# w3 times w_out summed row by row in all eight PSUM banks, and the first unit's gates put ahead of the rounding

## The chip, the cores and the metric

The kernel runs on one core of a Trainium2 chip. The metric is the device time of one execution in microseconds (us). The core has five engines with a queue each: TensorE (PE; its weight loads are shown apart as PEld), VectorE (DVE), ScalarE (ACT), GpSimd (POOL) and SyncE (SP), which here issues all the DMAs. Within one queue, instructions run in the order in which they were built.

## The reference

A gated linear recurrence over the sequence is followed by a feed-forward block without a nonlinearity.

```python
# q, k, v, a_re, a_im: (B=4, H=8, S=768, D=48); S_re, S_im: states of D x D for each head
mag = np.sqrt(a_re * a_re + a_im * a_im)
scale = np.minimum(mag, 0.999) / (mag + 1e-06)
a_re_n, a_im_n = (a_re * scale, a_im * scale)
for t in range(S):
    new_re = ar * S_re - ai * S_im
    new_im = ar * S_im + ai * S_re
    kv = np.einsum('bhd,bhe->bhde', k[:, :, t], v[:, :, t])
    S_re, S_im = (new_re + kv, new_im)
    y[:, :, t] = np.einsum('bhd,bhde->bhe', q[:, :, t], S_re)
# x: y with the heads beside each other, (3072, 384)
a = x @ w1              # (384, 1024)
b = x @ w2              # (384, 1024)
h = a * b @ w3          # (1024, 1024)
return (h @ w_out)      # (1024, 384)
```

The four weights come as 64-bit floats, everything else as 32-bit floats.

## The kernel before

**Units.** The sequences are cut into eight units of work, two halves of 384 steps (TT) for each of the four batches; a unit has three chunks of 128 steps. Each unit has two sides. Its gates (`gates`, L529 on) are elementwise: ACT and DVE turn re and im into running products of magnitudes and running sums of angles, and multiply them into q and k. The results are moved (L630) into the tiles KL and QL, which have heads in another place; twelve DMAs a unit. Then PE does the attention of the unit: transposes of the keys (`turn`, L650, copied out by ACT in L652), scores of a chunk (`scores`, L662, masked by DVE in L664), outputs (`outputs`, L689, copied by ACT to xT in L691) and states (`state`, L700, added up by DVE in L707). Two of the tiles, re and im, exist once, so that the next unit's loads wait for the last reader.

**The feed-forward block.** `ffn_ab` (L720) multiplies x by a block of w1 and one of w2, ACT copies the first (L725) and DVE multiplies (L726). Since nothing stands between w3 and w_out, the kernel multiplies those two once, into w3o (1024 by 384), and `ffn_out` (L736) multiplies by that. While PE does the attention of one unit, it does the feed-forward work of the unit before.

**Rounding.** 64-bit weights are loaded as pairs of 32-bit words into raw tiles of 8 KB a partition (three of them) and rounded to 32-bit floats by `convert`. For w3: two passes on ACT (L762, L764) and two on DVE (L766, L773). For the others: one on ACT (L768) and three on DVE (L769, L771, L773). ACT's result goes to the tile low, of which there is one.

**The start.** PE's order is written out by hand at the end of the function (a manual schedule); for the other engines the order comes from a scheduler that goes by the order of the program and by priority. The program loads the first column block of w3 in two halves, then the gates' inputs of unit 0, then w_out in four blocks of two rows, and then seven more column blocks of w3, each with 1 KB pieces. `fuse(j)` multiplies column block j by w_out in eight matmuls into one PSUM bank, in two parts of four, and ACT copies the bank to w3o (L847). Each of these matmuls is two in the trace. A column block needs all of w_out, so the first matmul of a block runs as soon as the rows it needs are rounded. Steps of the gates of unit 0 are put between the blocks. Blocks 0 to 5 go first on PE; blocks 6 and 7 are put as fill between the pieces of unit 0's attention.

**PSUM.** Eight banks are given out by name: two for scores (ps_s, tag sc), two for transposes, outputs and states (ps_v, tag v), four for the feed-forward block and for fuse (ps_m, tag mm).

**SP.** All loads and moves stand in one queue. A load of a raw tile waits until the rounding three loads before has read its tile.

Of the kernel before, what the change touches and what calls it, by code (L numbers as in the profile page):

```python
# [10 lines left out]
FP = mybir.dt.float32  # L11
# [4 lines left out]
AF = mybir.ActivationFunctionType  # L16
# [358 lines left out]
def kernel(  # L375
# [36 lines left out]
    nc = tc.nc  # L412
    B, H, D, S = qt.shape
    P = 128
    C = 128
    NC = S // C
    DM = H * D
    FF = w1.shape[1]
    KD = DM // P
    DG = P // H  # L420
    KF = FF // P
    WB = 2 * P
    HEAD = 6
    SPLIT1 = False
    TT = S // 2
    UC = TT // C
    NU = 2 * B
# [9 lines left out]
    w3o = weights_pool.tile([P, KF, DM], FP, name="w3o")  # L437
# [6 lines left out]
    one = fast.enter_context(tc.tile_pool(name="one", bufs=1))  # L444
    two = fast.enter_context(tc.tile_pool(name="two", bufs=2))
    ps_s = fast.enter_context(tc.tile_pool(name="ps_s", bufs=2, space=PSUM))
    ps_v = fast.enter_context(tc.tile_pool(name="ps_v", bufs=2, space=PSUM))
    ps_m = fast.enter_context(tc.tile_pool(name="ps_m", bufs=4, space=PSUM))
# [31 lines left out]
    def load_rows(dst, src, u, which=range(KD), queue=nc.sync):  # L480
        b, h = divmod(u, 2)
        for i, f in enumerate(which):
            queue.dma_start(out=dst[:, i, 0:TT], in_=src[b, :, DG * f:DG * (f + 1), h * TT:(h + 1) * TT].rearrange(
                "h d s -> d h s"))

    def load_gates(u):
        g = g_t.setdefault(u, {})
        for n, src in (("re", art), ("im", ait)):
            g[n] = one.tile([P, KD, TT], FP, tag=n, name=n)
            load_rows(g[n], src, u)  # L490

    def take_qk(u):
        g = g_t.setdefault(u, {})
        g["q"] = gate_pool[u % 2].tile([P, KD, TT], FP, tag="q", name="q")
        g["k"] = gate_pool[u % 2].tile([P, KD, TT + 1], FP, tag="k", name="k")

    def load_qkv(u):
        b, h = divmod(u, 2)
        if "q" not in g_t.get(u, {}):
            take_qk(u)  # L500
        g = g_t[u]
        load_rows(g["k"], kt, u)
        load_rows(g["q"], qt, u)


        vr = one.tile([P, UC, DM], FP, tag="vr", name="vr")
        nc.sync.dma_start(out=vr, in_=v[b, h * TT:(h + 1) * TT].rearrange("(c p) e -> p c e", p=C))
        g["vr"] = vr
# [20 lines left out]
    def gates(u, split):  # L529
# [6 lines left out]
        re, im, q = g["re"], g["im"], g["q"]  # L536
        K2 = g["k"]
        k, r = K2[:, :, 0:TT], R[:, :, 0:TT]
        parts = [slice(0, KD)]

        def act(**kw):
            chain(nc.scalar.activation(**kw))  # L542
# [55 lines left out]
        for s in parts:  # L598
            for f in range(s.start, s.stop):
                nc.vector.tensor_tensor_scan(  # L600
                    out=Z[:, f], data0=im[:, f], data1=im[:, f],
# [3 lines left out]
        for s in parts:  # L605
            n = re[:, s].bitcast(I32)
# [146 lines left out]
    def convert(dst, src, halves):  # L753
        r, m = dst.shape[1:]
        raw = cv["raw"].tile([P, r, m, 2], I32, tag="raw", name="raw")
        nc.sync.dma_start(out=raw.rearrange("p r m w -> p r (m w)"), in_=src)
        lo, hi = raw[:, :, :, 0], raw[:, :, :, 1]
        low = cv["low"].tile([P, r, m], I32, tag="low", name="low")
        b = dst.bitcast(I32)
        if halves:  # L760
            ends = low.rearrange("p r m -> p (r m)")
            nc.scalar.activation(out=ends.bitcast(U16)[:, 0::2].rearrange("p (r m) -> p r m", r=r), in_=lo.bitcast(U32),  # L762
                                 func=AF.Copy, scale=2.0 ** -29)
            nc.scalar.activation(out=ends.bitcast(BF)[:, 1::2].rearrange("p (r m) -> p r m", r=r), in_=hi.bitcast(FP),  # L764
                                 func=AF.Sign)
            nc.vector.tensor_scalar(out=b, in0=hi, scalar1=3, scalar2=None, op0=OP.logical_shift_left)  # L766
        else:
            nc.scalar.activation(out=low, in_=lo.bitcast(U32), func=AF.Copy, scale=2.0 ** -29)  # L768
            nc.vector.tensor_scalar(out=b, in0=hi, scalar1=3, scalar2=0x3FFFFFFF, op0=OP.logical_shift_left,  # L769
                                    op1=OP.bitwise_and)  # L770
            nc.vector.scalar_tensor_tensor(out=b, in0=hi, scalar=-0x40000000, in1=b, op0=OP.bitwise_and,  # L771
                                           op1=OP.bitwise_or)
        nc.vector.tensor_tensor(out=b, in0=b, in1=low, op=OP.add)  # L773

    def load_weight(dst, src, halves=False):
        if src.dtype == FP:
            nc.sync.dma_start(out=dst, in_=src)
        else:
            convert(dst, src, halves)

    def words(src):
        return (src if src.dtype == FP else src.bitcast(I32)).rearrange("(i p) m -> p i m", p=P)
# [27 lines left out]
    w3_t = {}  # L810

    def rounding():

        stack = ExitStack()
        for n, k in (("raw", 3), ("low", 1)):
            cv[n] = stack.enter_context(tc.tile_pool(name=n, bufs=k))
        return stack

    def columns(src, j0, j1):
        n = 1 if src.dtype == FP else 2  # L820
        return words(src)[:, :, n * j0:n * j1]
# [2 lines left out]
        return [lambda d=d, w=w, n=n: load_weight(d[:, n], columns(w, n * WB, (n + 1) * WB))  # L824
                for n in range(FF // WB) for d, w in ((w1s, w1), (w2s, w2))]

    def wo_work():
        w3_t["wo"] = one.tile([P, KF, DM], FP, tag="ab", name="wo_s")
        return [lambda i=i: load_weight(w3_t["wo"][:, i:i + 2], words(wo)[:, i:i + 2]) for i in range(0, KF, 2)]

    def w3_work(j, step=KF):
        w3_t[j] = two.tile([P, KF, P], FP, tag="xT", name="w3s")
        for f in range(0, KF, step):
            load_weight(w3_t[j][:, f:f + step], columns(w3t, j * P, (j + 1) * P)[:, f:f + step], True)

    def fuse(j):

        got = {}

        def part(f0):  # L840
            if f0 == 0:
                got["m"] = ps_m.tile([P, DM], FP, tag="mm", name="f")
            m = got["m"]
            for f in range(f0, f0 + KF // 2):
                nc.tensor.matmul(out=m, lhsT=w3_t[j][:, f], rhs=w3_t["wo"][:, f], start=(f == 0), stop=(f == KF - 1))  # L845
            if f0:
                nc.scalar.activation(out=w3o[:, j], in_=m, func=AF.Copy, scale=1.0 if w3t.dtype == FP else 2.0)  # L847
        return [lambda: part(0), lambda: part(KF // 2)]

    def judge():  # L850

# [50 lines left out]
    with tc.manual_schedule(engines={mybir.EngineType.PE}):  # L902

        phase = rounding()
        w3_work(0, KF // 2)
        load_gates(0)
        take_qk(0)
        steps = gates(0, True)
        for i, f in enumerate(wo_work()):
            f()  # L910
            if i >= 1:
                next(steps)
        w3_work(1)
        fill = fuse(0)
        for j in range(2, KF):
            if j == KF - 1:
                for _ in range(2):
                    next(steps, None)
            w3_work(j)
            if j == 2:  # L920
                load_qkv(0)
            for f in fill:
                f()
            fill = fuse(j - 1)
            next(steps, None)
            next(steps, None)
        work = w12_work()
        for f in work[:2]:
            f()
        for _ in steps:  # L930
            pass
        fill += fuse(KF - 1)
        load_gates(1)
        steps = gates(1, False)
        take_qk(1)
        rest = ffn(0, 2)
        work = work[2:]
        for i, p in enumerate(pieces(0)):
            for f in p:
                f()  # L940
            if i in (0, 1, 3, 5):
                fill.pop(0)()
            if i == 0:
                for f in work[:2]:
                    f()
                load_qkv(1)
            if i >= 2:
                next(steps)
            if i in (5, 7):
                work[2 + (i == 7)]()  # L950
        for i, f in enumerate(rest[:HEAD]):
            f()
            if i < 2:
                work[4 + i]()
            if i == 2:
                phase.close()
            next(steps)
        head_pool[1] = fast.enter_context(tc.tile_pool(name="late_heads", bufs=1))
        for _ in steps:
            pass  # L960
        load_gates(2)
        late = fast.enter_context(tc.tile_pool(name="late", bufs=2))
        look = check_weights(late)
        for u in range(1, NU):
            steps = gates(u + 1, False) if u + 1 < NU else iter(())
            unit(u, steps, rest[HEAD:] if u == 1 else ffn(u - 1), look if u > 1 else iter(()))
            for _ in steps:
                pass
            if u + 2 < NU:
                load_gates(u + 2)  # L970
        for _ in look:
            pass
        judge()
        for f in ffn(NU - 1):
            f()
# [41 lines left out]
```

## Time and profile before

| | us |
|---|---|
| median of 3 runs | 602.62 |
| lowest, highest | 602.47, 604.31 |
| the profiled execution | 604.26 |
| its span, from the first to the last instruction | 602.5 |
| PE busy | 554.6 (92%) |
| ACT busy | 345.4 (57%) |
| DVE busy | 300.0 (50%) |
| matmuls of w3 and w_out (L845), 128 of them | 46.7 |
| first of these matmuls starts | 17.16 |
| moves of unit 0 issued | 51.56 to 63.1 |
| first scores of unit 0 | 67.81 |
| first matmul with w1 | 95.44 |
| first scores of unit 1 | 136.03 |

The busy time of an engine is an average over stages with different limits, so a table by stage says more. In such a table a window of the span has one row, with the busy time of each engine. A view of waits says which instruction an engine stood waiting for. The chain of waits is followed back from the last instruction: at each step to what released it, or to the instruction before it on its engine. Matmuls are pipelined, and a matmul's duration is longer than the spacing from one to the next.

### The profile page before, as it was taken

What the parts mean: (1) busy time and instruction counts of PE and PEld (TensorE: products, weight loads), DVE (VectorE), ACT (ScalarE), POOL (GpSimd) and SP (SyncE); (2) the same over time, 40 slices, a digit from 0 to 9 for tenths busy, and PEclk for the clock granted to TensorE, in tenths of its full rate; (3) what the DMA queues carried; (4) which work ended last, traced back from release to release, by engine and by line L of the source; (5) the groups of instructions that cost most, each with busy time, mean ns of one, the idle gap of its engine ahead of it and who ended that gap; (6) DMA issues with size and microseconds to landing.
All of it is one profiled execution on the core that took longest, in us unless ns stands there. A gap on an engine that the chain in (4) does not pass through costs nothing.

```text
span 602.5 us, 8758 instructions
## 1 busy us (share of the span) xinstructions
PE 554.6 (92%) x3514; PEld 366.1 (61%) x3514; DVE 300.0 (50%) x388; ACT 345.4 (57%) x542; POOL 5.3 (1%) x11
## 2 busy tenths in 40 slices
PE   0599697959998999999999999999999999999996
PEld 0255584538755666667667766676567666766553
DVE  5988388744953664348324672477049602210110
ACT  5789476437484965588658986998375312101100
POOL 3000000000000000000000000000000000000000
PEclk9989898998999999999999999999999999999999
DMA  9996996373067268545744459735700430000001
GB/s 296 289 308 193 281 272 216 104 176 101 27 150 204 62 184 208 184 154 173 194 145 146 142 172 253 226 119 159 182 15 1 111 73 14 1 14 28 0 1 44
DMA packets 53025, 84.70 MB, mean 141 GB/s; under 512 B 4592, under 2 KB 44272, under 8 KB 52976
## 3 DMA queue, kind: packets, MB, share of 16 engines
q1 hardware_dynamic: 52976, 84.06, 49.1%
q8 instruction: 29, 0.48, 0.4%
q14 instruction: 20, 0.16, 0.1%
HBM read 60.42 MB, written 4.72 MB: 108 GB/s over the span
## 4 chain that ended last, share of the span: by engine, by line
PE 74%; DVE 9%; ACT 7%; DMA 5%; issue 2%; SPq 2%; ACTq 0%; DVEq 0%
PE m L720 36%; PE o L736 19%; PE sc L662 6%; PE y L689 5%; PE kv L700 4%; PE f L845 3%; DMA raw<-in_w_dram 2%; PE tp L650 2%; DMA QL<-q 2%; ACT re L542 1%; ACT gZ L542 1%; SPq L630 1%; ACT gR L542 1%; DVE w3s L773 1%; DMA look<-in_a_re_dram 1%
## 5 line engine op out<-in xcount | busy, mean ns | idle before, releaser
L720 PE MATMUL m<-xT,w1s 128*128 128x384 f32 x384 | 137.5, 495 | 5.3 <-ACT xT L691 5.3
L720 PE MATMUL m<-xT,w2s 128*128 128x384 f32 x384 | 134.3, 486 | 0.0
L736 PE MATMUL o<-w3o,ab 128*128 128x384 f32 x384 | 128.3, 489 | 0.0
L726 DVE TENSOR_TENSOR ab<-m,a 128x384 f32<-128x384 f32 x64 | 35.4, 554 | 150.5 <-PE m L720 141.0
L720 PEld LDWEIGHTS m<-xT,w2s 128*128 128x128 f32 x384 | 73.0, 190 | 51.0 <-issue 0.3
L736 PEld LDWEIGHTS o<-w3o,ab 128*128 128x128 f32 x384 | 71.4, 190 | 47.2 <-issue 1.4
L720 PEld LDWEIGHTS m<-xT,w1s 128*128 128x128 f32 x384 | 70.0, 192 | 46.6 <-ACT xT L691 6.5
L725 ACT COPY a<-m 128x384 f32<-128x384 f32 x64 | 30.4, 476 | 88.3 <-PE m L720 88.2
L845 PE MATMUL f<-wo_s,w3s 128*128 128x384 f32 x128 | 46.7, 518 | 21.7 <-DVE wo_s L773 19.3
L662 PE MATMUL sc<-QL,KL 96*128 96x128 f32 x384 | 51.2, 290 | 13.0 <-DMA QL<-q 10.0
L662 PEld LDWEIGHTS sc<-QL,KL 96*128 96x128 f32 x384 | 48.7, 202 | 19.7 <-issue 16.5
L845 PEld LDWEIGHTS f<-wo_s,w3s 128*128 128x128 f32 x128 | 24.8, 200 | 40.9 <-DVE wo_s L773 21.6
L652 ACT COPY KT<-tp 128x384 f32<-128x384 f32 x40 | 33.9, 848 | 26.3 <-PE tp L650 26.2
L664 DVE COPY_PREDICATED A<-causal,sc 128x512 f32<-128x512 int32 x48 | 34.0, 733 | 25.2 <-PE sc L662 24.8
L689 PE MATMUL y<-A,V 128*32 128x128 f32 x768 | 39.2, 275 | 0.6 <-DVE T L707 0.6
L689 PEld LDWEIGHTS y<-A,V 128*32 128x32 f32 x768 | 32.7, 109 | 9.4 <-issue 7.2
L689 PE MATMUL y<-QL,T 96*32 96x128 f32 x640 | 34.5, 272 | 0.0
L740 ACT COPY ot<-o 128x384 f32<-128x384 f32 x24 | 11.4, 476 | 40.1 <-PE o L736 40.1
L700 PEld LDWEIGHTS kv<-V,KT 128*96 128x96 f32 x320 | 29.8, 165 | 3.2 <-issue 1.8
L689 PEld LDWEIGHTS y<-QL,T 96*32 96x32 f32 x640 | 31.2, 110 | 0.0
L700 PE MATMUL kv<-V,KT 128*96 128x64 f32 x320 | 29.9, 246 | 0.0
L803 ACT ACTIVATE look<-look 128x512 f32<-128x512 f32 (+1 forms) x36 | 23.3, 654 | 10.3 <-DMA look<-in_w_dram 9.7
(98 smaller groups left out, 572.9 us busy)
## 6 DMA issues: line engine op xcount, KB each, us to landing
look<-in_w_dram SPq DMA_DIRECT2D x28, 512.0 KB, 4.8
raw<-in_w_dram SPq DMA_DIRECT2D x7, 1024.0 KB, 6.6
raw<-in_w_dram SPq DMA_DIRECT2D x8, 768.0 KB, 7.8
KL<-gR SPq DMA_DIRECT2D x24, 192.5 KB, 3.1
KL<-k SPq DMA_DIRECT2D x24, 192.5 KB, 3.8
re<-in_a_re_dram SPq DMA_DIRECT2D x24, 192.0 KB, 4.6
im<-in_a_im_dram SPq DMA_DIRECT2D x24, 192.0 KB, 3.9
k<-in_k_dram SPq DMA_DIRECT2D x24, 192.0 KB, 4.6
```

The costliest lines, as they stand in the source:

```text
L542: chain(nc.scalar.activation(**kw))
L652: nc.scalar.copy(out=KT_t[u, c][:, :, :, x].rearrange("p h d f -> p f d h"), in_=tp.rearrange("p f (d h) -> p f d h", h=H))
L662: nc.tensor.matmul(out=sc[:, j], lhsT=KL[:, x * n + j, w], rhs=QL[:, x * n + j, w], start=True, stop=True)
L664: nc.vector.copy_predicated(out=A[:, x * n:(x + 1) * n], data=sc, mask=causal.rearrange("p (h t) -> p h t", h=1).to_broadcast([P, n, C]))
L689: nc.tensor.matmul(out=o, lhsT=a, rhs=b, start=s0, stop=s1)
L700: nc.tensor.matmul(out=kv[:, hd], lhsT=KT[:, hd].rearrange("p d x f -> p (d x f)"), rhs=V[:, hd], start=True, stop=True)
L720: nc.tensor.matmul(out=m, lhsT=w[:, j * P // WB, f, j * P % WB:j * P % WB + P], rhs=xT_t[u][:, f], start=(f == 0), stop=(f == KD - 1))
L725: nc.scalar.copy(out=a, in_=got[0])
L726: nc.vector.tensor_tensor(out=ab_t[u][:, j], in0=got[1], in1=a, op=OP.mult)
L736: nc.tensor.matmul(out=m, lhsT=ab_t[u][:, f, t * P:(t + 1) * P], rhs=w3o[:, f], start=(f == 0), stop=(f == KF - 1))
L803: nc.scalar.activation(out=hi, in_=hi, func=AF.Square, scale=2.0 ** 15)
L845: nc.tensor.matmul(out=m, lhsT=w3_t[j][:, f], rhs=w3_t["wo"][:, f], start=(f == 0), stop=(f == KF - 1))
```

## The change

The multiplication of w3 and w_out is summed over rows instead of column blocks. A row of w3 here is a block of 128 partitions with all 1024 columns, 8 KB in one piece for each partition. `row_work(f)` loads and rounds row f of w3 and row f of w_out (384 columns, so that w_out comes in eight loads instead of four). The first row of w3 comes in two halves with w_out's row between them. `fuse(f, j)` is now one product: it adds row f's part to sum j. Eight sums are open at the same time, in all eight banks: two of tag sc, two of tag v and four of tag mm. Only after row 7 are they copied to w3o.

On PE, rows 0 to 5 go first with all eight products, then rows 6 and 7 with the products of sums 0 to 3; the products of rows 6 and 7 for sums 4 to 7 are the fill between the pieces of unit 0's attention, two at a time, at the same four places as before. The steps of unit 0's gates are emitted with high priority, two after each row, and all that are left before the last products; the copies to w3o have high priority too. The tile low has two buffers. The name SPLIT1, which nothing read, is replaced by SPLIT, an empty tuple, with which `parts` stays one slice.

```diff
-    SPLIT1 = False
+    SPLIT = ()
...
-        for n, k in (("raw", 3), ("low", 1)):
+        for n, k in (("raw", 3), ("low", 2)):
...
+    def row_work(f, parts=1):
+
+        if f == 0:
+            w3_t["wo"] = one.tile([P, KF, DM], FP, tag="ab", name="wo_s")
+        w3_t[f] = two.tile([P, FF], FP, tag="xT", name="w3s")
+
+        def some(n):
+            step = FF // parts
+            load_weight(w3_t[f][:, n * step:(n + 1) * step].rearrange("p (i m) -> p i m", i=1),
+                        columns(w3t, n * step, (n + 1) * step)[:, f:f + 1], True)
+        some(0)
+        load_weight(w3_t["wo"][:, f:f + 1], words(wo)[:, f:f + 1])
+        for n in range(1, parts):
+            some(n)
...
+    def fuse(f, j):
+        if not sums:
+            sums.extend([ps_s.tile([P, DM], FP, tag="sc", name="f") for _ in range(2)] +
+                        [ps_v.tile([P, DM], FP, tag="v", name="f") for _ in range(2)] +
+                        [ps_m.tile([P, DM], FP, tag="mm", name="f") for _ in range(4)])
+        nc.tensor.matmul(out=sums[j], lhsT=w3_t[f][:, j * P:(j + 1) * P], rhs=w3_t["wo"][:, f], start=(f == 0),
+                         stop=(f == KF - 1))
+        if f == KF - 1:
+            with tc.high_priority():
+                nc.scalar.activation(out=w3o[:, j], in_=sums[j], func=AF.Copy, scale=1.0 if w3t.dtype == FP else 2.0)
...
-        w3_work(0, KF // 2)
+        row_work(0, 2)
         load_gates(0)
         take_qk(0)
         steps = gates(0, True)
-        for i, f in enumerate(wo_work()):
-            f()
-            if i >= 1:
-                next(steps)
-        w3_work(1)
-        fill = fuse(0)
-        for j in range(2, KF):
-            if j == KF - 1:
-                for _ in range(2):
+        for f in range(KF):
+            if f:
+                row_work(f)
+            if f == 2:
+                load_qkv(0)
+            if f >= KF - 2:
+                continue
+            for j in range(KF):
+                fuse(f, j)
+            for _ in range(2):
+                with tc.high_priority():
                     next(steps, None)
-            w3_work(j)
-            if j == 2:
-                load_qkv(0)
-            for f in fill:
-                f()
-            fill = fuse(j - 1)
-            next(steps, None)
-            next(steps, None)
         work = w12_work()
         for f in work[:2]:
             f()
-        for _ in steps:
-            pass
-        fill += fuse(KF - 1)
+        with tc.high_priority():
+            for _ in steps:
+                pass
+        for f in range(KF - 2, KF):
+            for j in range(KF // 2):
+                fuse(f, j)
+        fill = [lambda f=f, j=j: [fuse(f, j + x) for x in range(2)] for f in range(KF - 2, KF) for j in range(KF // 2, KF, 2)]
```

As built, SP's queue has the loads of rows 0 to 5 first, with unit 0's inputs between them and, after row 4, the loads of unit 1's im and k and a third of its q; then the twelve moves of unit 0; and only then the loads of rows 6 and 7 and of w1 and w2. Before, all of w3 and the first block of w1 stood ahead of the moves, and unit 1's inputs behind them. On ACT and DVE the two last gate stages of unit 0 stand ahead of the rounding of rows 5 to 7. From the moves of unit 1 on, the order of loads is the same as before.

More of the change, by code (lines that the diff above doesn't have):

```diff
@@ L538, in gates @@
         k, r = K2[:, :, 0:TT], R[:, :, 0:TT]
-        parts = [slice(0, KD)]
+        parts = [slice(f, f + 1) for f in range(KD)] if u in SPLIT else [slice(0, KD)]
         def act(**kw):
@@ L825, in w12_work @@
                 for n in range(FF // WB) for d, w in ((w1s, w1), (w2s, w2))]
[L827 to L848, printed above, removed]
+    def row_work(f, parts=1):
[10 more added lines that the diff above has]
+            some(n)
+    sums = []
+    def fuse(f, j):
[8 more added lines that the diff above has]
+                nc.scalar.activation(out=w3o[:, j], in_=sums[j], func=AF.Copy, scale=1.0 if w3t.dtype == FP else 2.0)
     def judge():
```

## The prediction

> **What bounds the kernel now.** I read the busy table first, then a table by stage, the waits of PE, and the chain of waits.
>
> ```profile
> 29.00:60.00 31.00, 30.65 (x91) 17.79 (x92) 25.75 (x35) 28.45 (x32) 0.00 (x0) 0.94 0.81 251
> 60.00:68.00 8.00, 3.39 (x14) 1.88 (x13) 2.52 (x3) 2.13 (x3) 0.00 (x0) 1.00 1.05 280
> 68.00:96.00 28.00, 23.39 (x285) 20.00 (x285) 20.34 (x27) 17.27 (x22) 0.00 (x0) 0.93 1.05 292
> ...
> 136.00:186.00 50.00, 45.78 (x375) 32.72 (x376) 28.84 (x32) 30.34 (x45) 0.00 (x0) 0.96 0.42 109
> 186.00:602.00 416.00, 410.62 (x2638) 271.62 (x2636) 173.48 (x224) 229.65 (x396) 0.00 (x0) 1.00 0.40 113
> ```
>
> Columns: window, length, busy PE, PEld, DVE, ACT, POOL, granted clock, DMA share, GB/s. From 186 us on PE is full, with work that the change leaves alone. A gain can only come from making that stage start earlier.
>
> ```profile
> PE f L845 <- DVE wo_s L773: 19.3, 4, 17.2
> PE sc L662 <- DMA QL<-q: 10.0, 2, 5.4
> PE m L720 <- ACT xT L691: 5.3, 2, 4.0
> PE sc L662 <- DMA out_dram<-ot: 3.0, 1, 3.0
> ```
>
> These are PE's waits (total, times, longest). Two are for QL: unit 0's scores at 67.81 and unit 1's at 136.03.
>
> ```profile
> 62.57 5.00 DMA QL<-q
> 67.81 3.53 PE sc L662 x16
> ...
> 86.25 7.77 DMA raw<-in_w_dram
> 94.11 0.91 ACT low L768
> 95.44 13.53 PE m L720 x36
> ...
> 116.66 1.37 DVE gZ L608
> ...
> 131.15 4.58 DMA QL<-q
> 136.03 3.75 PE sc L662 x16
> ```
>
> The chain passes through unit 0's moves, a w1 block, and then unit 1's gates. From 94 to 115.6 us DVE idles about 1 us in all, so those gates share a full DVE with the last four w1/w2 blocks. Everything after 136 us hangs on that QL: unit 2's re is loaded behind unit 1's moves and starts unit 2's gates, whose QL holds PE again at 185. So the end follows the instant at which unit 1's gates finish, not the instant at which unit 0's do.
>
> **What the Trainium skill says.** "DMA: Bandwidth & Descriptors", section "Anatomy of one DMA": semaphore waits are taken by the issuing sequencer, and DMA engines only consume their queues. The trace agrees: SP stood 10.8 us in five waits for L766, with everything behind it unissued. Same page, "Specifications": 512 B and more run at line rate, so 1 KB pieces should lose nothing against 8 KB. The trace differs a little: 1 KB pieces of w3 ran at 348 GB/s (34 to 40 us), 3 KB pieces of w_out at about 400 (11 to 14 us). "TensorE: Matmul & The Clock Gate", "HAM oscillation": idle gaps above some 3.4 us bring the slow clock back. It agrees: after 4.6 us idle the 16 score matmuls took 3.53 us, after 2.95 us idle 2.02. "PSUM — Partial Sum Buffer", "The four PSUM rules": an output fills at most one of eight banks; eight open sums leave none for a transpose. No trace here shows that yet.
>
> **The change, step by step.** I replay the changed kernel's built instruction order by hand, with the spacing of like instructions in this trace: L762 and L764 1.21 us each (a w3 row 2.42 on ACT), L766 0.6, L773 1.15; gate passes of 1152 elements 1.07 on ACT, 1.27 on DVE; a scan 0.93; KT copy 0.65; L768 0.82; a move's issue 0.62.
>
> Unknown first: a 384-element w_out rounding. On DVE it costs at least half of the 768 form (2.3/2 = 1.15 us) and at most all of it (2.3). I take 1.35, so eight rows cost 1.6 more than four pairs (0 to 9). The cover is the 8 us in which DVE waits for row 6, below; without it that 1.6 lands in the gates. The second low buffer lets ACT run a row ahead (three waits on L773, 3.3 us in all, in the view of raw); it is in the replay. SPLIT replaces an unused name: nothing.
>
> *Gates of unit 0.* ACT gets r0a, wo0, r0b, then re, which 0.39 MB of w_out has pushed from at most 8.35 to about 9.3. L762 of row 1 stands before the first gZ pass and waits for row 1 (about 14.0), so that pass goes from 13.54 to 15.2, and the Exp before the scans ends at 22.7 (20.44 before). From there the rounding steps aside: scans end 26.2 (27.6), Arctan starts 30.0 (36.7), L600 ends 35.2 (43.0), the last Sin ends 44.0 (54.4). The twelve moves are issued from 43.6 to 51.9 (51.56 to 63.1). Eleven us are won for unit 0.
>
> *And given back.* On SP the load of row 6 stands behind all twelve moves, although its raw slot is free near 42. Issued at 52.0 behind 2.4 MB of moves (250 GB/s, as at 62 to 66 us), it lands at 58.5. With three raw slots shared by rows of w3 and w_out, row 7 lands at 62.2 and the last w_out row at 64. ACT, idle from 49 to 58.5, ends row 7 at 64.9, DVE at 66.6. PE has rows 6 and 7 for four sums (8 x 0.65 = 5.2 us) ahead of its first transpose, and the transposes and scores need banks that only the w3o copies free: row 7's four matmuls end 69.2, the fourth copy 69.7. With 0.35 per transpose and 1.3 per pair of fills, scores start at 72.6 instead of 67.81, with 2.6 us of fills left instead of 5.2. PE is 2.2 us behind at this place. Behind the waiting transpose stand all of PE; behind the waiting w3o copies on ACT stand KT, low of w2 and unit 1's first Ln.
>
> *Unit 1.* Its im, k and a third of q were loaded early (1.4 MB), but rows 6 and 7 (2.9 MB) now fall into the busy stretch. From the moves' end to the last needed w1 block 11.7 MB have to land: 2.9 MB of rows at 400 GB/s (done at 63.2, bound by their issues), 8.85 MB at the 290 of 68 to 96 us: 30.5 us, plus 1.5 to land: 95 (94.05 for an earlier block before). ACT runs from 69.7 nearly without a gap: 22 operations, about 18 us, plus some 3.5 of waits for w1/w2 blocks, vr and L567. Unit 1's Exp before the scans ends 91.2 (87.6), L574 stands behind unit 0's third A and T on DVE and ends 93.8. The third xT comes at 96.2 behind that block, PE m at 96.3 (95.44).
>
> But of the four late w1/w2 blocks two were rounded before. After L574 DVE has one L773 (0.87), three scans (2.65), L710, L588, L585, L586, L589 (5.7), three ab (1.45), the last two blocks (4.45, which includes two L769) and the L600 scans (2.8): 17.9 us, plus 0.6 waiting for gR. L600 ends at 112.3 instead of 115.5, L616 starts at 117.4 instead of 120.54, the scores of unit 1 at 132.8 instead of 136.03. PE comes to them at about 128, so it waits for QL as before, and PE's 1.5 us wait before it (122.0) goes. Sum: -3.2 us. The later order of instructions is the same, so the shift stays.
>
> The profiled execution took 604.26 us, 602.5 of span and 1.76 around it: 601.1 after. The median of the runs shown, 602.62, is 1.64 less: **599.4**.
>
> **Rivals.** B, the transfers hide it: between 60 and 96 us DMA is full (share 1.05). At 350 GB/s for rows and 270 for the rest (the stretch 60 to 75 had 278) the last w1 block lands at 97.5, the third xT and gR's Ln are 2.6 late, the sum is -0.6: 602.0. For it: the full share. Against: wider pieces, and 1.4 MB moved to an idle time.
>
> C, slower: row 6 behind the moves. If SP issues the twelve at the old pace (11.5 us) and the row takes the old median landing of raw blocks (7.5 us), it lands at 62.6, 4.1 late, and PE, idle for over 4 us, starts row 6 on the slow clock (+1.7, as at 95.44 where six took 3.84 instead of 2.10). ACT's long run begins at 75.5 instead of 69.7: -3.2 + 5.8 = +2.6, 605.2. The fourth w3o copy decides: no gain from 72.9, slower than can be taken for noise from 74.7. For it: the moves were issued one by one behind DVE before. Against: the products now come in one run.
>
> D, the front is better than replayed: rows land 2 us sooner and w_out rounding costs its lower bound. All of ACT's run shifts: 597 to 594.5.
>
> That the sums do not take all eight banks, or the gates keep their place, is excluded by the built order.
>
> **How the numbers follow.** A (599.4, own range 597 to 601.5) 0.44, B 0.20, C 0.31, D 0.05. About 0.3%, 1.8 us, is what a measurement of this kernel can tell from none. Faster: 0.41 of A and all of D, 0.46. Same: 0.03 of A and 0.18 of B, 0.21. Slower: C and 0.02 of B, 0.33. The range runs from 595 (half of D left out) to 606.5 (the far side of C left out).
>
> **What would show it.** Moves issued from about 44 to 52; a gap of some 9 us on ACT before row 6's L762, ended by raw; the first transpose on PE after row 7, near 69.5; L616 of unit 1 near 117 and its scores near 133, PE m near 96. Wrong: moves later than 48 (the replay of the front), a fourth w3o copy after 73 (C), raw ending ACT's waits between 75 and 98 for more than 6 us (B).

## The result, and the profile after

The changed kernel took 610.48 us (median of 4 runs, 609.25 to 611.63), the kernel before 603.46 us in the runs beside it. The ratio is 1.0105, 95% interval 1.0056 to 1.0154: slower by about 1%. The profiled execution took 609.83 us, with a span of 608.0 (before 604.26 and 602.5). The forecast of 599.4 us and its range, up to 606.5, were wrong.

The table by stage, with the windows that the prediction showed of before (columns: window, length, busy PE, PEld, DVE, ACT, POOL, granted clock, DMA share, GB/s):

```profile
29.00:60.00 31.00, 23.17 (x63) 13.00 (x64) 23.54 (x37) 18.73 (x20) 0.00 (x0) 0.89 0.90 262
60.00:68.00 8.00, 1.39 (x4) 0.53 (x3) 3.91 (x6) 4.25 (x5) 0.00 (x0) 0.72 0.66 248
68.00:96.00 28.00, 23.93 (x206) 17.75 (x208) 21.28 (x28) 21.36 (x31) 0.00 (x0) 0.93 0.99 279
...
116.00:136.00 20.00, 18.93 (x63) 10.87 (x61) 12.62 (x16) 9.70 (x12) 0.00 (x0) 1.00 0.59 146
136.00:186.00 50.00, 45.05 (x366) 32.72 (x367) 28.28 (x31) 30.29 (x45) 0.00 (x0) 0.93 0.40 101
186.00:602.00 416.00, 413.26 (x2645) 274.20 (x2644) 174.32 (x225) 228.41 (x395) 0.00 (x0) 1.00 0.41 115
```

The last stage is as full as before, so nearly all of the loss is from ahead of it. Between 29 and 60 us ACT was busy 18.73 us instead of 28.45 and PE 23.17 instead of 30.65; the clock from 60 to 68 us fell to 0.72.

The waits of PE in the whole span (total, times, longest):

```profile
PE f L850 <- DVE wo_s L773: 28.1, 6, 8.6
PE sc L662 <- DMA re<-in_a_re_dram: 4.8, 1, 4.8
PE sc L662 <- DMA out_dram<-ot: 2.7, 1, 2.7
PE m L720 <- ACT xT L691: 1.8, 2, 1.2
PE y L689 <- ACT KT L652: 1.7, 1, 1.7
PE tp L650 <- ACT w3o L854: 1.3, 1, 1.3
```

The second line is the wait for unit 1's QL, now at 139.71. The view names re because that load, issued after the moves, was the last DMA event before it. The last line answers what the prediction left unseen: with all eight banks taken, the first transpose stood for a copy to w3o. The chain of waits (start, length, what):

```profile
48.16 6.10 DMA KL<-gR
...
54.32 8.44 DMA raw<-in_w_dram
...
66.31 6.87 DMA raw<-in_w_dram
...
76.47 11.22 DMA vr<-in_v_dram
...
102.94 23.50 PE m L720 x72
...
134.75 4.95 DMA re<-in_a_re_dram
```

The first two lines are the step that failed: a move of unit 0, then row 6's load, issued at 54.32 behind all the moves. The third is w1's first block and the fourth unit 1's vr, whose copy stands ahead of unit 1's gates on ACT. ACT's timeline shows who stood for it (start, length, instruction, and in brackets the idle time before and what ended it):

```profile
51.10 0.54 ACT L768 ACTIVATE low<-raw 128x384 int32<-128x384 uint32 x1
62.84 1.35 ACT L762 ACTIVATE low<-raw 128x1024 uint16<-128x1024 uint32 x1 [11.20 <-DMA raw<-in_w_dram]
...
73.26 0.93 ACT L768 ACTIVATE low<-raw 128x768 int32<-128x768 uint32 x1 [3.60 <-DMA raw<-in_w_dram]
74.09 1.61 ACT L854 ACTIVATE w3o<-f 128x384 f32<-128x384 f32 x4
76.03 0.84 ACT L652 COPY KT<-tp 128x384 f32<-128x384 f32 x1 [0.32 <-PE tp L650]
...
78.98 1.16 ACT L542 ACTIVATE gA<-re 128x1152 f32<-128x1152 f32 x1 [0.58 <-DMA re<-in_a_re_dram]
```

ACT stood 11.20 us for row 6 and 3.60 us for w1's first block, whose rounding stands ahead of the copies to w3o in its order. The fourth copy ended at 75.7, and unit 1's first Ln (gA<-re) came at 78.98 instead of 72.62. From there the delay goes through: L616 of unit 1, the multiplication after its last Sin with which its moves can begin, at 124.83 (120.54 before), its scores at 139.71 (136.03), unit 2's scores at 189.70 (185.25), the end at 608.0 (602.5).

### The profile page after: what moved, and what is told of

Read it like the earlier page. It is cut to its first block, busy times and chain, and to the rows that moved or that the text cites. A ratio compares the mean times of both kernels' runs of the same rounds, so it can differ in the third digit from the quotient of the medians.

```text
span 608.0 us, 8781 instructions
## 1 busy us (share of the span) xinstructions
PE 560.9 (92%) x3514; PEld 370.6 (61%) x3514; DVE 301.5 (50%) x400; ACT 344.0 (57%) x546; POOL 5.3 (1%) x11
## 4 chain that ended last, share of the span: by engine, by line
PE 76%; DMA 10%; ACT 5%; DVE 5%; SPq 1%; issue 1%; ACTq 0%; DVEq 0%
PE m L720 40%; PE o L736 18%; PE sc L662 7%; DMA raw<-in_w_dram 6%; PE y L689 6%; PE kv L700 4%; DMA vr<-in_v_dram 2%; PE tp L650 2%; DMA KL<-gR 1%; ACT gZ L542 1%; DMA re<-in_a_re_dram 1%; ACT re L542 1%; ACT low L762 1%; DVE gZ L600 1%; DMA out_dram<-ot 1%
## 5 line engine op out<-in xcount | busy, mean ns | idle before, releaser
L720 PE MATMUL m<-xT,w1s 128*128 128x384 f32 x384 | 135.9, 490 | 1.8 <-ACT xT L691 1.8
L720 PEld LDWEIGHTS m<-xT,w2s 128*128 128x128 f32 x384 | 73.0, 190 | 50.9
L736 PEld LDWEIGHTS o<-w3o,ab 128*128 128x128 f32 x384 | 71.4, 190 | 47.2 <-issue 1.6
L850 PE MATMUL f<-wo_s,w3s 128*128 128x384 f32 x128 | 52.0, 565 | 28.1 <-DVE wo_s L773 28.1
L850 PEld LDWEIGHTS f<-wo_s,w3s 128*128 128x128 f32 x128 | 27.6, 223 | 49.7 <-DVE wo_s L773 31.4
```

Of the source, the lines that this page charges most:

```text
L720: nc.tensor.matmul(out=m, lhsT=w[:, j * P // WB, f, j * P % WB:j * P % WB + P], rhs=xT_t[u][:, f], start=(f == 0), stop=(f == KD - 1))
L736: nc.tensor.matmul(out=m, lhsT=ab_t[u][:, f, t * P:(t + 1) * P], rhs=w3o[:, f], start=(f == 0), stop=(f == KF - 1))
L850: nc.tensor.matmul(out=sums[j], lhsT=w3_t[f][:, j * P:(j + 1) * P], rhs=w3_t["wo"][:, f], start=(f == 0), stop=(f == KF - 1))
```

## The experiments

The change has three parts that can be made alone: the second buffer of low, the rows with their eight open sums, and the gates ahead. Three theories stood at first. Order: what stands behind what on SP. Bank: the open sums keep the transposes waiting. Size: smaller pieces and more loads. Times are medians; ratios are against runs of the kernel before on the same chip. Some kernels have one to three lines more ahead of a place, so that L616 is L617 there; the text uses the names of the kernel after.

**Rows alone, gates alone, low alone.**

```diff
# rows_only: the kernel after
-                with tc.high_priority():
-                    next(steps, None)
+                next(steps, None)
# gates_only: the kernel before
-        for n, k in (("raw", 3), ("low", 1)):
+        for n, k in (("raw", 3), ("low", 2)):
-                next(steps)
+                with tc.high_priority():
+                    next(steps)
# low2: the kernel before
-        for n, k in (("raw", 3), ("low", 1)):
+        for n, k in (("raw", 3), ("low", 2)):
```

(In the first two the same is done at each place where a step of unit 0's gates is taken. Both have the second low buffer.)

> The whole change without the part that puts unit 0's gates ahead: rows, eight sums, single w_out rows remain. Order theory: most of rows 6 and 7 is loaded before the moves, the moves go out near 52 to 63 as in the kernel before, and the time is 601 to 605. Bank theory: the transposes wait for row 7's sums all the same, with banks as the reason, 606 to 611. Size theory: the smaller pieces cost here too, DVE and ACT are busier before 60 us by the w_out pieces, 606 to 611.

> The kernel before, whose w3o blocks are finished one by one and leave banks free, with the gates of unit 0 ahead of the rounding and two buffers of low. Order theory: the moves go out near 44 to 54 and the last two column blocks of w3 stand behind them on SP, so the last w3o copy is late, ACT idles for some 8 us near 54 to 62, and unit 1's chain starts late: 606 to 611, much as with the whole change. Bank theory: the transposes need no bank of a sum, PE goes on to unit 0's scores near 66, and the time is no more than that of the kernel before, 598 to 603. Size theory: no row pieces here, so 598 to 603 too.

> The kernel before with a second buffer of low and nothing else of the change. Prediction's term: ACT saves its three waits on L773 (3.3 us in all) but the moves depend on the gates, which ACT reaches a little sooner: 601 to 604. If the second buffer lets rounding run ahead of the gates on ACT instead, so that the gates come later: 604 to 607.

Rows: 608.70 us, ratio 1.0097 (1.0064 to 1.0131). Gates: 611.75 us, 1.0145 (1.0112 to 1.0178). Low: 601.71 us, 0.997 (0.995 to 0.999), faster than the changed kernel and, by a little, than the kernel before. With it, unit 1's first Ln came 2.6 us earlier (70.02) and L616 4.5 us earlier (116.04): ACT goes on to the next block's low while DVE still adds the last one. So on top of the second buffer, by the ratios, rows cost some 8 us, gates ahead some 11, and both together some 8: each part loses alone, and they share the loss. The bank and size theories wanted gates without rows to be no slower than before, and fell there as the main cause. The order theory was right on gates, but it wanted rows alone at 601 to 605. In rows alone one move was issued at 54.35, then SP stood before full raw slots, and eleven moves went out from 61.52 to 69.35: the moves behind the rows cost as much as the rows behind the moves.

**Row 6 ahead, the moves on another queue, the moves behind the rows.**

```diff
# row6_first: the load of w3's row 6 alone
+        with tc.high_priority() if ahead else ExitStack():
             nc.sync.dma_start(out=raw.rearrange("p r m w -> p r (m w)"), in_=src)
# moves_pool
-                    nc.sync.dma_start(out=dst[x * KD + f::2 * KD], in_=src[x][:, f])
+                    (nc.gpsimd if split else nc.sync).dma_start(out=dst[x * KD + f::2 * KD], in_=src[x][:, f])
# moves_late
+                    go = lambda x=x, f=f: nc.sync.dma_start(out=dst[x * KD + f::2 * KD], in_=src[x][:, f])
+                    held.append(go) if split else go()
...
+        with tc.high_priority():
+            for _ in steps:
+                pass
+        for f in held:
+            f()
         for f in work[:2]:
             f()
-        with tc.high_priority():
-            for _ in steps:
-                pass
```

> Order theory (the load of row 6 stands behind unit 0's twelve moves on SP, and all that follows is late because of that): the load goes out near 45 us instead of 54.3 and lands near 52, the moves end about 1 us later than 53.9; row 6 is rounded near 54 and PE multiplies it then; row 7's load still goes out behind the moves and lands near 62, so the fourth w3o copy comes near 70 instead of 75.3 and the time falls to 603 to 606. Bank theory (eight open sums keep the transposes behind row 7, whatever is loaded when): row 7 sets the first transpose, which moves by less than 2 us, and the time stays at 608 to 611. Size theory (pieces of 1 KB, more loads, the slow clock): DMA is as full as before, 608 to 611.

> The whole change, with unit 0's twelve moves issued from GpSimd's queue instead of SP's. Order theory: the moves still go out near 44 to 54, but row 6's load goes out as soon as its raw slot is free, near 45 to 48, and row 7's near 52; row 7 is rounded by 62, the fourth w3o copy comes near 67 and unit 1's gates end 5 us earlier than in the change or more: 597 to 602. Bank theory: the transposes still wait for row 7's eight sums, 604 to 608. Size theory: the queue is not what is scarce, DMA is as full, 607 to 611.

> The whole change, the gates' arithmetic still ahead, but eleven of unit 0's twelve moves issued after the loads of rows 6 and 7 and of their w_out rows. Order theory: row 6 goes out near 44, row 7 near 53 and lands near 61, its w_out row by 63; the moves go out from about 55 to 62 and land by 67; the fourth w3o copy comes near 68 to 70 instead of 75.3, unit 0's scores near 71 to 73 instead of 78.74, the time is 602 to 606. Bank theory and gate theory: no gain over the change, 608 to 611.

Row 6 ahead: 608.99 us, ratio 1.0077 (1.0048 to 1.0106). It did not isolate what it should. In the traced execution, which took 613.44 us, w3's row 6 was being rounded at 53.94, but now w_out's row 6 stood behind the moves and came to ACT at 65.95; the first w3o copy came at 73.75.

Moves on GpSimd's queue: 638.31 us, 1.0589 (1.0557 to 1.0621). Row 6 went out at 44.32, but with moves and loads in flight together w_out's row 6 took 17.82 us to land (52.18 to 70.00), and the scheduler put unit 1's gates ahead of unit 0's key copies on ACT: PE stood 28.2 us in one wait for KT.

Late moves: 610.94 us, 1.0108 (1.0066 to 1.0151). This is the run that decides on the order theory. The front did what the order theory said: the fourth w3o copy ended near 68.3, the scores of unit 0 started at 71.85 and PE's first matmul with w1 at 96.43, close to the kernel before. The time did not move. ACT's waits from 65 to 102 us in it (total, times, longest):

```profile
ACT V L515 <- DMA vr<-in_v_dram: 6.2, 2, 4.8
ACT low L770 <- DMA raw<-in_w_dram: 4.8, 2, 3.3
```

With the moves issued until 65.4, unit 1's re, vr and the w1 blocks went out late, and ACT stood before them, in order, ahead of unit 1's gates: first Ln at 79.89, L616 at 126.24. The wait for the rows had been exchanged for waits for unit 1's transfers. Bank: the transposes went as soon as the copies, so banks alone don't explain the time either.

**w_out ahead, and the fill behind the scores.**

```diff
# wo_first: the kernel after
-        load_weight(w3_t["wo"][:, f:f + 1], words(wo)[:, f:f + 1])
+        if f == 0:
+            for i in range(0, KF, 2):
+                load_weight(w3_t["wo"][:, i:i + 2], words(wo)[:, i:i + 2])
# gates_latefill: gates_only
-            if i in (0, 1, 3, 5):
+            if i in (2, 3, 5, 6):
                 fill.pop(0)()
```

> The whole change, but w_out is loaded and rounded in its four pairs at the start, as in the kernel before, so that only whole rows of w3 follow and no w_out row of 384 KB takes one of the three raw slots; eight sums and gates ahead as in the change. In the built order all rows of w3 then stand ahead of the moves on SP. Order theory, with the slots as its reason: row 7 lands before 58, the fourth w3o copy comes before 68 instead of 75.3, unit 0's scores start at 70 or earlier instead of 78.74, the time is 598 to 604. Bank theory: the transposes wait for row 7 as before, 607 to 611. Gate theory (rounding put back behind the gates leaves PE and DMA idle between 30 and 45 us, which is the loss in all three variants so far): DMA share at 30 to 45 us stays near 0.8 and the time at 606 to 610.

> The kernel before with unit 0's gates ahead and two buffers of low, and, unlike that experiment, the products of the last two column blocks put behind unit 0's first scores on PE. Order theory, in which the products ahead of the scores matter: scores start near 67 to 70 instead of 77.9, the third xT by 98, time 602 to 607. Gate theory (the products that had no rounded blocks before 50 us have to be done later anyway, and ACT stands behind their copies): scores earlier, but unit 1's gates as late as before, 608 to 612.

w_out ahead: 611.25 us, 1.0105 (1.0071 to 1.0138). No w_out row took a slot any more and all rows of w3 were issued before the moves, which went out from 54.48. But the fourth w3o copy ended at 72.7, not before 68: PE multiplied from 54.57 to 72.2 without a pause, after 27 us of waits for rounded rows. First matmul with w1 at 95.72, as before; L616 at 125.14, as in the change. Fill behind the scores: 612.45 us, 1.0145 (1.0118 to 1.0171); unit 0's scores at 66.35, 11.5 us earlier than with gates alone, and no gain. In all variants with gates ahead or rows, the DMA share from 30 to 45 us was 0.73 to 0.83, against 0.98 before and 1.07 with the second low buffer: rounding put back frees raw slots later, and the loads stand. That lag was made up, though: over the first 60 us the change moved 272 GB/s, as before, and PE was busy 38.55 us (38.25), while ACT had done 9.1 us less and DVE 5.0 us less.

**Unit 1's gates ahead too.** By now every slower run but the one with the moves on GpSimd's queue had a later L616 of unit 1 than the kernel before, and the faster run an earlier one, so unit 1's first Ln was pulled forward by loading re early.

```diff
# re1_early: the kernel after; re1_late: the same on moves_late
         with tc.high_priority():
             for _ in steps:
                 pass
+        with tc.high_priority():
+            load_gates(1)
# low2_re1: low2, the same place in the kernel before
```

(The old call is taken out; in the first two the lines that set up unit 1's gates and its tiles for q and k move up with it.)

> The kernel with the late moves of unit 0, and besides it unit 1's re is loaded ahead: right behind the first move, before rows 6 and 7 are finished, instead of behind the moves and a w1 block. Revised theory (what sets the end is L616 of unit 1, and that is late in every slow variant because its first Ln comes at 76 to 82 us instead of 72.62, re standing behind rows and moves on SP): the first Ln starts before 65, L616 comes before 105 instead of 120.54, PE no longer waits before unit 1's scores, which start near 130 to 133, and the time is 597 to 602. Rival (PE's own work is late: the third xT and the w1 blocks set the end whatever the gates do): L616 early, scores of unit 1 at 137 or later, 605 to 610.

> The whole change with nothing but unit 1's re loaded ahead, behind the first of unit 0's moves; in the built order all of unit 1's gates then stand ahead of row 6's rounding on ACT and DVE, in the stretch in which both idled for row 6. Revised theory: L616 comes before 85, but row 6 is rounded only behind it, so that the w3o copies come near 88 and PE is the bound: unit 1's scores at 140 to 150, 608 to 618. If rows behind the moves cost nothing beside the late gates: 598 to 604.

> The kernel before with the second buffer of low and unit 1's re loaded behind the second of unit 0's moves; nothing else of the change. Revised theory: unit 1's first Ln starts about 5 us earlier than the 70.02 of the second buffer alone, its gates are no longer interleaved with the w1 and w2 blocks, L616 comes before 105 instead of 116.04, and PE goes to unit 1's scores without a wait (it waited some 6 us before them): 595 to 600. Rival (the moves, put back by the load between them, and the w1 blocks, put back behind the gates, cost as much as the gates win): 600 to 606.

On the late moves 624.49 us (ratio 1.0381, 1.0318 to 1.0443), on the change 627.41 us (1.0398, 1.0348 to 1.0448) and on low2 622.06 us (1.0322, 1.0269 to 1.0375): much slower, against my expectation for the first and the third, and beyond it for the second. L616 came early in all three (90.03, 84.49 and 103.95), unit 1's scores late (149.24, 155.07 and 146.74). In re1_late L616 was 30 us earlier than before, and PE's first matmul with w1 came at 117.52. The waits of PE in it:

```profile
PE tp L652 <- ACT KT L654: 20.4, 2, 15.9
PE y L691 <- DVE T L709: 4.0, 2, 3.1
PE y L691 <- ACT KT L654: 3.6, 1, 3.6
```

The gates are a chain that goes back and forth between ACT and DVE. With all of it next in ACT's order, unit 0's key copies stood behind it, and PE behind them. So the end has two conditions, and this breaks the second: L616 early, and PE fed on the way.

**DVE's full stretch.** From L574, the step ahead of unit 1's first scans, to L616 DVE is the fullest of the engines that the gates use: busy 20.40 of 23.74 us in the change (ACT 13.24). Here work is taken out of it, or a wait out of ACT's order. (The V copies move in every unit; noadd and low2_noadd leave the low part of these weights out.)

```diff
# noadd: the kernel after; low2_noadd: low2. For the blocks n >= 2 of w1 and w2
-        nc.vector.tensor_tensor(out=b, in0=b, in1=low, op=OP.add)
+        if add:
+            nc.vector.tensor_tensor(out=b, in0=b, in1=low, op=OP.add)
# low2_pooladd: low2
+        (nc.vector if add else nc.gpsimd).tensor_tensor(out=b, in0=b, in1=low, op=OP.add)
# late_vpool: moves_late; low2_vpool: low2
-            nc.scalar.copy(out=V[:, :, :, i, e0:e0 + D], in_=vr[:, :, :, i])
+            nc.gpsimd.tensor_copy(out=V[:, :, :, i, e0:e0 + D], in_=vr[:, :, :, i])
```

> The whole change without the last addition of the rounding (L773) in the four late blocks of w1 and w2, so that the low part is left out of these weights: 4 times 0.87 us less of DVE in the stretch in which it is full. If the end follows unit 1's gates and these follow DVE's sum: L616 about 3.5 us earlier than 124.83, unit 1's scores at 136 to 137 instead of 139.71, the time 3 to 4 us less, 606 to 608. If transfers or PE's own work set them: no change, 609 to 612.

> The kernel before with the second buffer of low, without the same four additions. If the end follows unit 1's gates and these follow DVE: L616 about 3 us earlier than 116.04, the time 2 to 3.5 us less than with the second buffer alone, 598 to 600. Otherwise 601 to 603.

> The kernel with the late moves, with the copies V<-vr made by GpSimd instead of ACT, so that ACT no longer stands before vr (1.39 and 4.78 us) ahead of unit 1's gates. If (a) transfers bind through ACT's order: unit 1's Exp before the scans ends 4 to 7 us earlier than 101.2, L616 before 122 instead of 126.24, the time 603 to 607. If (b): L616 later than 124, 608 to 612.

> The kernel before with the second buffer of low and the copies V<-vr on GpSimd. ACT loses four copies of 0.6 us and its waits for vr ahead of unit 1's later passes; if that reaches unit 1's gates, 598 to 601; if GpSimd's copies are slow enough to hold the state products on PE, or slow DVE, 602 to 606.

> The kernel before with the second buffer of low, and the additions L773 of the four late blocks of w1 and w2 on GpSimd instead of DVE. If DVE's sum before unit 1's gates decides and GpSimd works beside it: L616 near 113 instead of 116.04, the time 598.5 to 600.5. If GpSimd's additions hold the raw buffers or slow DVE's own passes: L616 at 116 or later, 601 to 606.

Without the four additions the change took 607.08 us (1.0058, 1.003 to 1.0087) and low2 599.0 us (0.9937, 0.991 to 0.9964): by the ratios 2.8 us less than the change (0.0047 of 603 us) and 2.0 less than low2 (0.0033). The intervals touch or overlap, so the times alone don't prove it. The traces agree: from L574 to L616 it took 20.7 us instead of 23.7, and in low2 27.3 instead of 30.9, near the 3.5 us taken out. In low2's pair, though, the traces don't carry this to the end: unit 1's scores came 2.6 us earlier (128.89), unit 2's did not (181.42, against 181.33). (The first w3o copy was also 2.8 us earlier in noadd's trace, which the edit can't have made; row 6 landed at 60.09 there instead of 62.76: that is how far two executions can differ.)

Late moves with the V copies on GpSimd: 609.35 us, 1.0108 (1.0068 to 1.0149). L616 moved from 126.24 to 123.56, less than expected, and the time can't be told from that of the late moves. Its PE is the clearest sign of what sets the end: the first matmul with w1 started at 92.76, 2.7 us earlier than in the kernel before, and then:

```profile
PE tp L652 <- DVE gR L617: 8.8, 1, 8.8
```

PE was early and stood 8.8 us for unit 1's gates. On low2 the same edit gave 603.10 us, 1.0005 (0.9982 to 1.0029), no gain.

The additions on GpSimd: 603.78 us, 0.9991 (0.9972 to 1.001), no gain, and L616 at 116.00, as in low2. Two timelines of that kernel, GpSimd's and DVE's, of the same microseconds, show why:

```profile
90.99 2.34 POOL L773 TENSOR_TENSOR w1s<-w1s,low 128x768 int32<-128x768 int32 x1 [85.12 <-DVE w1s L771]
...
103.87 2.00 POOL L773 TENSOR_TENSOR w1s<-w1s,low 128x768 int32<-128x768 int32 x1 [4.43 <-DVE w1s L771]
```

```profile
91.62 2.13 DVE L769 TENSOR_SCALAR w2s<-raw 128x768 int32<-128x768 int32 x1
...
104.11 2.57 DVE L600 TENSOR_TENSOR_SCAN gZ<-im,st_ang 128x384 f32<-128x384 f32 x1
...
107.46 1.00 DVE L600 TENSOR_TENSOR_SCAN gZ<-im,st_ang 128x384 f32<-128x384 f32 x1
```

The pass of 0.56 us took 2.13 and the scan of 1.00 took 2.57 while GpSimd added. With two more such passes DVE lost 5.3 us, more than the 3.5 it was spared.

**All of it in one table**, in the order of L616 (traces in us, ratio with its interval above):

| | first matmul with w1 | unit 1: first Ln | L616 | scores | ratio |
|---|---|---|---|---|---|
| low2_noadd | 92.02 | 70.70 | 112.75 | 128.89 | 0.9937 |
| low2 | 91.38 | 70.02 | 116.04 | 131.47 | 0.997 |
| noadd | 101.57 | 75.60 | 120.40 | 135.66 | 1.0058 |
| before | 95.44 | 72.62 | 120.54 | 136.03 | 1 |
| gates_latefill | 98.35 | 77.32 | 122.58 | 139.01 | 1.0145 |
| rows_only | 99.88 | 78.15 | 122.83 | 137.78 | 1.0097 |
| late_vpool | 92.76 | 78.56 | 123.56 | 137.93 | 1.0108 |
| after | 102.94 | 78.98 | 124.83 | 139.71 | 1.0105 |
| wo_first | 95.72 | 81.48 | 125.14 | 140.11 | 1.0105 |
| gates_only | 103.30 | 76.56 | 125.59 | 140.76 | 1.0145 |
| moves_late | 96.43 | 79.89 | 126.24 | 141.38 | 1.0108 |

The scores of unit 1 come 14.4 to 16.4 us after L616 in each, whatever PE did before. From these scores to the end of the span it was 466.5 us (before) to 470.9 (wo_first); that rest of some 4 us is not explained by unit 1's gates, and it is as large as some of the differences to be explained: noadd has L616 where the kernel before has it and is 0.6% slower.

## Why the prediction was wrong

*The bound* was read rightly in the main: unit 1's scores follow the instant at which unit 1's gates finish, with the condition that re1_late added, and the end follows these scores to within some 4 us.

*Gates of unit 0*: nearly right. The last Sin ended at 45.2 (44.0), the moves went out from 44.79 to 53.9 (43.6 to 51.9). The unknown price of a 384-element rounding was 0.36 + 0.56 + 0.55 = 1.47 us (1.35 taken).

*And given back* is the step that failed, by its size. Its mechanism, the load of row 6 behind all twelve moves, is there:

| | predicted | measured |
|---|---|---|
| row 6 issued, landed | 52.0, 58.5 | 54.32, 62.8 |
| row 7 rounded on DVE | 66.6 | 71.2 |
| fourth w3o copy | 69.7 | 75.7 |
| scores of unit 0 | 72.6 | 78.74 |
| unit 1's Exp before the scans ends | 91.2 | 98.2 |
| L574 ends | 93.8 | 101.8 |
| L600 ends | 112.3 | 119.5 |
| L616 of unit 1 | 117.4 | 124.83 |
| scores of unit 1 | 132.8 | 139.71 |

Of the 6.0 us at the fourth copy, 4.3 come from the landing of row 6: 2.3 from the issue, 1.9 from a landing of 8.4 us where 6.5 had been taken. The estimate had the moves alone ahead of row 6. But row 5 and its w_out row, issued at 40.79 and 41.61, were still under way when the moves began, and landed at 48.6 and 50.1; the moves landed behind them, the first at 50.9 and the last at 60.5, and row 6 behind the moves. (In noadd's trace row 5 landed 2.5 us earlier, and row 6 2.7 us earlier, so that part of the 4.3 may belong to this one execution.) Another 0.3 came until row 7 was rounded, 4.6 us late. The rest is 0.4 on PE and 1.0 on ACT:

```profile
67.17 7.00 PE L850 MATMUL f<-wo_s,w3s 128*128 128x384 f32 x16 [6.61 <-DVE wo_s L773]
75.47 0.52 PE L650 MATMUL tp<-ident,gR 128*128 128x128 f32 x3 [1.30 <-ACT w3o L854]
```

```profile
70.63 0.55 DVE L773 CUSTOM_DVE_ANT_0 wo_s<-wo_s,low 128x768 uint16<-128x768 uint16 x1
```

PE's last product ended at 74.17, 3.0 us after row 7's rounding instead of 2.6. It had finished sum 0 at 72.2, but ACT, waiting for w1's first block, began the four copies only at 74.09, behind L768: a wait that the prediction had put at nothing. The slow clock was there, and cost little: after 6.61 us without work PE took 4.3 us for row 6's eight matmuls (67.17 to 71.4) instead of 2.6, but row 7 was rounded only at 71.2.

From the fourth copy to L574 the delay grew by 2 us, and at unit 1's scores it was 6.9: the terms after it, some 3.5 us of waits on ACT and 18.5 us of DVE from L574 to L600's end, were right (3.6 and 17.7 us measured). "PE m at 96.3" and "PE comes to them at about 128" fell with it: 102.94 and 134.9.

The price of a landing was on the page of the kernel before: raw blocks of w3 took a median of 6.6 us to land and those of w1 and w2 7.8. The one issued right behind the moves, at 63.23, took 7.5, and the three issued between 25 and 32 us, with the DMA engines full, 9.8 to 10.7. The 6.5 taken was below all of these. In the change the median of a w3 row is 8.7 us.

*Unit 1*: with 6.9 us more at its scores, the sum of -3.2 became +3.7. Another 1.8 us came behind it: 0.8 up to unit 2's scores, and 1.0 from there on, where those scores took 3.63 us on the slow clock instead of 2.02. The gap before them was 2.74 us, shorter than the 2.95 us after which the kernel before kept the full clock. The figure of some 3.4 us, which fitted the gaps that the prediction looked at, does not fit this one, and the measurement decides. The rest of the miss is the reference: the profiled execution of before lay 1.64 us above the median then shown, which the forecast took off; that of after lies 0.65 below its median.

*The rivals.* C was what happened, with the fourth copy past its 74.7 and row 6 landing at its 62.6. That its copy at 75.5 was nearly met is luck in part: its 1.7 us for the slow clock lay under the wait for row 7, and 0.3 of landing, 0.4 of PE and 1.0 of ACT's wait for w1's block stood in their place. Its 605.2 was too small, since it put 5.8 us on unit 1's gates where there were 6.9, and nothing later. B, the transfers, was hardly seen in the change (raw ended 0.6 us of ACT's waits between 75 and 98, and the 3.60 just ahead), but it was waiting: the late moves took C's delay away, and B's waits for raw and vr took its place, with the same time. So an early fourth copy is not enough. Whether it would gain together with early moves wasn't tried: no run had both, and none with rows or with gates ahead was faster than before.

*Where the expected gain went.* The 9 us by which unit 0's last Sin came earlier were real and bought nothing. By 45 us DVE had been busy 34.25 us in the change and 34.87 before: the gates had only changed places with the rounding. But the rounding is what frees raw slots for loads and feeds PE, and behind it stand unit 1's gates. What stays open is the share of each: which of the loads of unit 1, the raw slots and DVE's idle time between 45 and 68 us (10.6 us after, 7.6 before) made the delay at unit 1's first Ln, 3 to 9 us in the slower variants of the table, was not separated. One suspect has no run: unit 1's im, k and a third of q, loaded ahead of row 5 and not used before 81 us, took time of the DMA engines ahead of the rows.

## What to carry to other kernels

Before moving a chain ahead, ask what the end waits for: here the second unit's gates, so the first unit's were brought forward for nothing, while the work that they displaced was on the path. Where loads and SBUF-to-SBUF moves share one in-order queue and a few slots, changing the order swaps one wait for another; take the time of a landing from loads that were issued while others were still under way. Test the parts alone: the one part that gained (a second small buffer, 2 us) had been hidden under two that lost 8 and 11.

## What the runs showed of the hardware

GpSimd beside DVE is not free: int32 additions of 768 elements took 2.0 to 4.1 us on GpSimd (0.87 on DVE), and four of DVE's passes were stretched by 1.0 to 1.6 us each beside them. The Trainium skill, "SBUF — State Buffer", section "SBUF: two separate sides", calls the port pair that the two share an exclusive lock: whichever starts first has it for its whole instruction. The trace agrees in kind: beside the three short additions DVE passes stood. During that of 4.1 us (95.36 to 99.44) DVE's passes up to 98.1 ran at full speed, so that the addition seems to have stood for them, and then L586 took 2.51 us instead of 1.35.

Two queues added little bandwidth: with the moves on GpSimd's queue, 274 GB/s were moved from 45 to 60 us, in the change 266, and a load of 384 KB took 17.82 us to land, where the median in the change was 5.9. The skill's "DMA: Bandwidth & Descriptors", section "Rules for kernel authors", says that spreading DMAs over issuing engines saves issue time alone, since all run on the same 16 engines; the trace agrees: the DMA share was 1.01 from 45 to 60 us in that run, and 1.03 in the change.

The width of the pieces counted. The 1 KB pieces of w3 in the kernel before were moved at 348 GB/s (34 to 40 us, DMA share 1.09), the pieces of 8 and 3 KB in the change at 421 (13 to 16 us, DMA share 1.03). So 1 KB pieces did lose, a sixth of the rate, as the two figures in the prediction (348 and about 400) already showed. The faster loads bought no time here.
